# A list scheduler with new prices and a spare tile in three rings: attention and a gated channel mixer on one core

## The chip, the cores and the metric

The kernel runs on one core of a Trainium2 chip, with its five engines: TensorE (PE), VectorE (DVE), ScalarE (ACT), GpSimd (POOL) and SyncE (SP, which issues DMAs). The metric is the device time in microseconds; lower is better. Weights, inputs and the output lie in HBM.

## The reference

Attention with RMS-normalised q and k, then a channel mixer: tokens are blended with the token before, a squared ReLU and a sigmoid gate follow. B = 8, H = 12, S = 448, head size 64, D = 768, F = 1024, all float32 (the mixer's weights come as float64).

```python
def rmsnorm(x, g):
    return x / np.sqrt(np.mean(x * x, axis=-1, keepdims=True) + 1e-06) * g
q_n, k_n = rmsnorm(q, g_q), rmsnorm(k, g_k)
attn = softmax(1/sqrt(64) * q_n @ k_n.T)            # per batch and head
x = (attn @ v) laid out as (B, S, 768)
x_prev = x shifted by one token, zeros first
xk = mu_k * x + (1 - mu_k) * x_prev
xr = mu_r * x + (1 - mu_r) * x_prev
k = np.maximum(xk @ w_k, 0.0)
out = sigmoid(xr @ w_r) * (k * k @ w_v)
```

## The kernel before

All large products run in f16 as a high and a low part, three products for one (high by high, high by low, low by high). Work on attention goes by quads of heads: there are 24 quads `u` (three for each batch). `load` brings q and k, `stats` forms the norms (square on ScalarE, half the sum on GpSimd, the rest and a Newton inverse root on VectorE), `preps` scales, splits and transposes them into `stk`: for the first PE_T = 6 quads by TensorE's transposition through a PSUM bank (`turn`), later by a transposing DMA issued by SyncE. `scores` takes 7 groups for each quad; a group takes two of the 5 banks of the ring `sc`, and `expo` runs twice on it: VectorE finds the negated maximum, ScalarE the exponential with its sum in an accumulator. `probs` waits for both, forms the reciprocals and spawns two `split`s: ScalarE writes the high part into a `nat` tile, VectorE the low part and gives the score bank back. A transposing DMA then writes it to `pT`; ten early groups go by TensorE's transposition instead (`probs_pe`). `attends` multiplies with v and writes `x`.

The mixer follows, one batch at a time: `mix` blends two tokens (GpSimd into a `df` tile, VectorE onto it, ScalarE's high part, GpSimd's low part), `moe` runs the products, `square` forms the squared ReLU (ScalarE into a `kf` tile, ScalarE's square, GpSimd's square and low part), `gate` and `store` make the output tile `o`. `weights` and `wsplit` turn the float64 weights into two f16 parts; the staging tiles `wf` and `raw` of this work lie in a pool of their own. When the first `o` tile is taken, `late()` closes that pool and opens another in its place.

The order of every engine's instructions is not written by hand: each of these routines is a thread that yields instructions, and `Plan` is a list scheduler that emits them. It keeps a planned clock for each engine, the planned end of each use of a tile, and prices (`price`, and in `emit` those of DMAs and of TensorE's groups). In each step `run` takes, from all threads, the instruction with the smallest key: the later of its engine's clock and the end of what it depends on, less a tenth of its thread's priority. The emitted order is the order of the engine's queue. A thread that needs a tile of a `Ring` waits until one is free. Before the change, a VectorE instruction with no operand in PSUM is held in the plan until 190 ns before the planned end of the last GpSimd instruction emitted. A transposition on TensorE is priced 300 ns (`TR_COST`). The rings `nat`, `df` and `kf` have 4, 2 and 2 tiles (`NAT_BUFS`, the `df` ring's own figure and `KF_BUFS`).

Every instruction is recorded at one line of the profile, L256 (the call in `emit`), so groups are told apart by their tiles.

Of the kernel before, what the change touches and what calls it, by code (L numbers as in the profile page):

```python
# [87 lines left out]
LEAD_W = 1  # L88
PE_P = range(1, 21, 2)
SC_KEEP = 2  # L90
TR_COST = 300
W_GAP = 10e3
W_PUSH = 0.03
NEWTON_ON = "DVE"
# [1 line left out]
DMA_SLOW = 1.0  # L96
DMA_SHARE = 1.0
PE_SLOW = 1.0
F64_EXP = 2.0 ** -112
F64_NEG = -2.0 ** 32  # L100

# [45 lines left out]
def width(x):  # L147
    n = 1
    for _, c in x.ap[1:]:
        n *= c  # L150
    return n


def in_psum(x):
    return "PSUM" in str(x.tensor.space)
# [37 lines left out]
class Plan:  # L193
    LAT = 35

    def __init__(self, tc):
        self.tc = tc
        self.clk = dict.fromkeys(("PE", "DVE", "ACT", "POOL", "SP"), 0.0)
        self.last, self.use, self.threads = {}, {}, []
        self.form, self.dma_free, self.pool_end, self.n = None, {"SP": 0.0, "ACT": 0.0}, 0.0, 0  # L200

    def margin(self, form):
        if form == "moe":
# [46 lines left out]
    def emit(self, ops):  # L250
        e = ops[0].eng
        rel = self.ready(ops)
        s = max(self.clk[e], rel)
        for op in ops:
            with self.tc.issue_after(self.last[e].ins) if e in self.last else nullcontext():
                r = op.fn(op.kw["out"], op.kw["value"]) if op.fn.__name__ == "memset" else op.fn(**op.kw)  # L256
            self.last[e] = r
        if e == "PE":
            form, cost = ops[0].form
            form = MODE.get(form, 0)  # L260
            cost *= PE_SLOW
            if form != self.form:
                s += 105
            self.form = form
            self.clk[e] = s + cost
            fin = s + cost + 190
            for op in ops:
                self.note(op, fin)
        elif ops[0].fn.__name__.startswith("dma"):
            op = ops[0]  # L270
            x = op.kw["out"]
            n = width(x) * x.ap[0][1]
            if "transpose" in op.fn.__name__:
                w, iss, tot = n / 128 * 1.21, 1510, 4000
            else:
                w, iss, tot = n / 55, 600, 3300
            w, tot = w * DMA_SLOW, tot * DMA_SLOW
            other = "ACT" if e == "SP" else "SP"
            if e == "ACT":
                end = s + (375 if n > 60000 else 610)  # L280
            else:
                end = max(s + iss, min(self.dma_free[e] - 1200, s + 4000))
            self.clk[e] = end + 35
            begin = max(self.dma_free[e], s + tot - w - 900)
            both = DMA_SHARE * min(w, max(0.0, self.dma_free[other] - begin))
            self.dma_free[e] = begin + w + both
            self.dma_free[other] += both
            self.note(op, self.dma_free[e] + 900)
        else:
            op = ops[0]  # L290
            pace, dur = (x * OP_SLOW for x in price(op))
            if e == "DVE" and not any(in_psum(x) for x in op.kw.values() if isinstance(x, bass.AP)) and width(op.kw["out"]) > 2:
                s = max(s, self.pool_end - 190)
            self.clk[e] = s + pace
            if e == "POOL":
                self.pool_end = s + dur
            self.note(op, s + dur)
        self.n += 1

    def run(self):  # L300
        while self.threads:
            best, key = None, None
            for th in list(self.threads):
                if not isinstance(th[2], list):
                    if not th[2]():
                        continue
                    self.advance(th)
                    if th not in self.threads or not isinstance(th[2], list):
                        continue
                slack = self.margin(th[2][0].form[0]) if th[2][0].eng == "PE" else 0  # L310
                mode = MODE.get(th[2][0].form[0], 0) if th[2][0].eng == "PE" else None
                wait = SWITCH if mode == 0 and self.form else 0
                k = max(self.clk[th[2][0].eng] + wait, th[3] + slack) - PS * (th[1]() if callable(th[1]) else th[1])
                if best is None or k < key:
                    best, key = th, k
            if best is None:
                if any(isinstance(th[2], list) or th[2]() for th in self.threads):
                    continue
                assert not self.threads, [(th[0].__name__, th[2]) for th in self.threads]
                break  # L320
            r = self.ready(best[2])
            if r > best[3] + 1:
                best[3] = r
                continue
            self.emit(best[2])
            self.advance(best)


class Ring:
    def __init__(self, pool, shape, dtype, name, n, plan):  # L330
        self.pool, self.shape, self.dtype, self.name, self.plan = pool, shape, dtype, name, plan
        self.free, self.of, self.lent = ["%s%d" % (name, k) for k in range(n)], {}, {}

    def lend(self, owner, views):
        self.free = views + self.free
# [9 lines left out]
    def get(self, early=False):  # L345
        ok = lambda: [x for x in self.free if early or isinstance(x, str)]
        while not ok():
            yield ok
        tag = ok()[0]
        self.free = [x for x in self.free if x is not tag]  # L350
        if not isinstance(tag, str):
            self.of[id(tag)] = (tag, None, tag)
            return tag
        pool = self.pool() if callable(self.pool) else self.pool
        t = pool.tile(self.shape, self.dtype, name=tag, bufs=1)
        name = aps(t).tensor.name
        self.of[id(t)] = (tag, name, t)
        old = self.plan.use.get("slot " + tag)
        if old:
            self.plan.use[name, 0], self.plan.use[name, 1] = [(0, 1 << 30, old, True, False)], [(0, 1 << 30, old, True, False)]  # L360
        return t
# [27 lines left out]
def attn_moe_kernel(tc, q, k, v, g_q, g_k, mu_k, mu_r, w_k, w_v, w_r, out):  # L389
# [13 lines left out]
    T, V, A, G_, SP = (Engine(n, e) for n, e in (("PE", nc.tensor), ("DVE", nc.vector), ("ACT", nc.scalar), ("POOL", nc.gpsimd), ("SP", nc.sync)))  # L403
# [26 lines left out]
    st = {"wdone": 0, "g": 0, "moe": 0, "vl": 0, "gm": False, "mus": False, "want": "xk", "sg": 0, "su": 0, "pu": 0, "vi": 0, "wkeys": 0, "kdone": 0, "zq": 0, "tq": 0, "lu": 0}  # L430
# [7 lines left out]
    def until(f):  # L438
        while not f():
            yield f  # L440
# [4 lines left out]
    late_pool = []  # L445

    def late():
        if not late_pool:
            bctx.close()
            late_pool.append(ctx.enter_context(tc.tile_pool(name="late", bufs=1)))  # L450
        return late_pool[0]

    R = {
        "qk": Ring(ap_, [P, 2, S], F32, "qk", QK_BUFS, plan),
        "nat": Ring(ap_, [P, 2 * NT, P], F16, "nat", NAT_BUFS, plan),
        "stk": Ring(ap_, [P, 2, 2 * NT, P], F16, "stk", STK_BUFS, plan),
        "vh": Ring(ap_, [P, 2 * NSL, HD], F16, "vh", VH_BUFS, plan),
        "vl": Ring(ap_, [P, 2 * NSL, HD], F16, "vl", VH_BUFS, plan),
        "x": Ring(ap_, [P, NT + 1, HD], F32, "x", X_BUFS, plan),
        "xk": Ring(mp, [P, ND, 2, S], F16, "xk", 1, plan),  # L460
        "df": Ring(mp, [P, S], F32, "df", 2, plan),
# [469 lines left out]
    def wsplit(nm, kt, c, ci, f):  # L931
# [24 lines left out]
        st["wdone"] += 1  # L956
        st["wkeys"] += ci < NF
        if ci < NF and st["wkeys"] == NF:
            yield V.tensor_reduce(out=wsc[:, 0:1], in_=WSC[:, 0:NF], axis=AX.X, op=ALU.min)
            yield V.tensor_scalar(out=RSC, in0=WIN[:, 0:NF], scalar1=wsc[:, 0:1], scalar2=RELU_SCALE, op0=ALU.mult, op1=ALU.mult)  # L960
            yield V.tensor_reduce(out=wsc[:, 1:2], in_=WIN[:, 0:NF], axis=AX.X, op=ALU.max)
            yield V.scalar_tensor_tensor(out=wsc[:, 1:2], in0=wsc[:, 1:2], scalar=1.0 / RELU_SCALE, in1=smu[:, 0:1], op0=ALU.mult, op1=ALU.mult)
            st["rsc"] = True
        if st["wdone"] == NW:
            yield V.tensor_scalar(out=WIN[:, NF:NF + ND], in0=WIN[:, NF:NF + ND], scalar1=smu[:, 1:2], scalar2=0.5, op0=ALU.mult, op1=ALU.mult)
            yield V.tensor_scalar(out=WIN[:, NF + ND:NW], in0=WIN[:, NF + ND:NW], scalar1=wsc[:, 1:2], scalar2=0.5, op0=ALU.mult, op1=ALU.mult)
            yield V.tensor_scalar(out=WIN[:, NF + ND:NW], in0=WIN[:, NF + ND:NW], scalar1=wsc[:, 1:2], scalar2=None, op0=ALU.mult)
            st["wout"] = True
# [141 lines left out]
```

## Time and profile before

| | before |
|---|---|
| median of 3 runs | 1060.49 us (1059.37 to 1060.85) |
| the profiled execution's own time | 1058.49 us |
| its span | 1056.7 us |
| mean granted TensorE clock | 0.953 |
| busy PE / DVE / ACT / POOL | 925.9 / 802.9 / 770.7 / 675.8 us |
| the 16 DMA engines, HBM read and written | 50.40 and 11.01 MB |

The profile shows one execution. Busy time is the time in which an engine has an instruction under way; register, branch and DMA-issuing instructions do not count. A wait is the idle time of an engine ahead of an instruction, put down to what released it last. In a row of a group, `out<-in` names the tiles (buffer numbers left out), followed by the shapes and the count, then the busy time in us and the mean duration in ns, then the idle time just before these instructions and its releasers. In a row of one tile the three figures are the least, middle and greatest duration in ns, followed by the first and the last start in us. `x126` is a count. In the rows by stage the engines' busy times stand in the order PE, PEld (weight load), DVE, ACT, POOL, followed by the granted clock, the DMA engines' share and GB/s.

### The profile page before, as it was taken

The page shows a single profiled execution, that of the slowest core. Times are in us where ns is not written, and L with a number is a line of the kernel's source. Part 1 is how long each engine was busy: PE and PEld are TensorE (multiplying, and loading weights), DVE is VectorE, ACT ScalarE, POOL GpSimd, SP SyncE. Part 2 cuts the span into 40 slices and gives each one's busy share as a digit, 9 for nine tenths or more (in the row PEclk, how much of TensorE's full clock was granted, in tenths as well). Part 3 has the DMA queues.
Part 4 walks back from the last instruction along what each step waited for, and adds up shares of the span by engine and source line. Part 5 has one row for each costly group of instructions (what it writes and reads, how often), then busy time and mean ns, then how long its engine had stood idle before and what let it go on. Part 6 is the DMA issues. An engine that isn't in the chain of part 4 may idle for free. (4 is left out here: it accounts for less than half of the span.)

```text
span 1056.7 us, 19126 instructions
## 1 busy us (share of the span) xinstructions
PE 925.9 (88%) x6185; PEld 488.9 (46%) x6185; DVE 802.9 (76%) x2034; ACT 770.7 (73%) x1786; POOL 675.8 (64%) x716
## 2 busy tenths in 40 slices
PE   1667666889988999998989999999899999999997
PEld 1334323444544555454534455455445554455564
DVE  5888899898699688868997897959876898673100
ACT  3687877888679788877788787868787888773311
POOL 2575579655588576874698457857695569725711
PEclk9567878899999999999999999999999999999999
DMA  6865557876877899778976998679887898753011
GB/s 172 196 145 123 136 140 189 176 145 134 178 134 146 163 172 165 155 149 148 176 160 129 181 174 165 136 143 183 151 152 153 165 179 164 135 89 79 1 31 30
DMA packets 467108, 151.68 MB, mean 144 GB/s; under 512 B 438848, under 2 KB 463424, under 8 KB 467008
## 3 DMA queue, kind: packets, MB, share of 16 engines
q1 hardware_dynamic: 447472, 132.47, 66.1%
q10 hardware_dynamic: 19536, 18.00, 5.9%
q8 instruction: 48, 0.79, 0.3%
q14 instruction: 52, 0.43, 0.1%
HBM read 50.40 MB, written 11.01 MB: 58 GB/s over the span
## 5 line engine op out<-in xcount | busy, mean ns | idle before, releaser
L256 PE MATMUL mm<-wvh,kk 128*128 128x384 f16 x896 | 233.3, 326 | 0.5 <-DVE o L256 0.5
L256 ACT ACTIVATE sc<-sc,sums 128x448 f32<-128x448 f32 x316 | 192.2, 611 | 54.1 <-DVE sums L256 47.1
L256 DVE SCALAR_TENSOR_TENSOR nat<-sc,sums,nat 128x448 f16<-128x448 f32 x306 | 199.8, 676 | 37.0 <-ACT nat L256 35.3
L256 PE MATMUL mm<-xk,wkh 128*128 128x448 f16 x768 | 213.1, 359 | 9.7 <-DVE WSC L256 5.7
L256 ACT ACTIVATE nat<-sc,sums 128x448 f16<-128x448 f32 (+1 forms) x326 | 194.9, 646 | 25.8 <-DVE sums L256 10.4
L256 DVE TENSOR_REDUCE sums<-sc 128x1 f32<-128x448 f32 x336 | 193.6, 614 | 21.9 <-PE sc L256 21.3
L256 PE MATMUL mm<-wrh,xr 128*128 128x384 f16 x672 | 177.1, 326 | 0.0
L256 PEld LDWEIGHTS <-kk 128*128 128x128 f16 (+1 forms) x1362 | 129.5, 98 | 97.2 <-issue 15.6
L256 PE MATMUL sc<-stk 64*128 64x448 f16 (+1 forms) x1152 | 128.3, 369 | 34.4 <-DVE nat L256 19.4
L256 PE MATMUL mm<-wvl,kk 128*128 128x384 f16 x448 | 146.0, 326 | 0.0
L256 PE MATMUL mm<-xk,wkl 128*128 128x448 f16 x384 | 137.8, 359 | 0.0
L256 PE MATMUL ot<-pT,vh 128*64 128x448 f16 x768 | 122.4, 376 | 17.3 <-DMA pT<-nat 8.0
L256 PEld LDWEIGHTS <-xr 128*128 128x128 f16 x1008 | 95.6, 98 | 73.4 <-issue 13.1
L256 DVE SCALAR_TENSOR_TENSOR df<-x,bsc,df 128x448 f32<-128x448 f32 x96 | 108.3, 1137 | 25.3 <-POOL df L256 25.0
L256 PEld LDWEIGHTS <-wkh 128*128 128x128 f16 x768 | 72.8, 99 | 83.9 <-issue 25.5
L256 PE MATMUL mm<-wrl,xr 128*128 128x384 f16 x336 | 109.5, 326 | 0.0
L256 PEld LDWEIGHTS <-stk 64*128 64x128 f16 (+1 forms) x1152 | 43.5, 99 | 103.3 <-issue 68.5
L256 POOL TENSOR_TENSOR o<-o,bsc 128x384 f32<-128x384 f32 x48 | 43.8, 913 | 69.5 <-DVE o L256 57.0
L256 POOL TENSOR_TENSOR nat<-nat 128x448 f32<-128x448 f32 x46 | 53.9, 1171 | 50.6 <-ACT nat L256 45.4
L256 POOL TENSOR_TENSOR qk<-qk,ss 128x896 f32<-128x896 f32 x36 | 62.5, 1737 | 34.5 <-DVE ss L256 28.8
L256 DVE SCALAR_TENSOR_TENSOR o<-o,mm 128x384 f32<-128x384 f32 x56 | 30.6, 546 | 70.2 <-PE mm L256 70.2
L256 POOL TENSOR_TENSOR nat<-qk,nat 128x896 f16<-128x896 f32 x36 | 67.8, 1883 | 23.4 <-ACT nat L256 23.3
(141 smaller groups left out, 1632.6 us busy)
## 6 DMA issues: line engine op xcount, KB each, us to landing
out_dram<-o SPq DMA_DIRECT2D x56, 192.0 KB, 3.3
qk<-in_k_dram SPq DMA_DIRECT2D x46, 224.0 KB, 4.0
qk<-in_q_dram SPq DMA_DIRECT2D x108, 64.0 KB, 2.5
vf<-in_v_dram SPq DMA_DIRECT2D x96, 64.0 KB, 2.8
raw<-in_moe_w_v_dram ACTq DMA_DIRECT2D x12, 512.0 KB, 4.7
vf<-in_v_dram SPq DMA_DIRECT2D x96, 48.0 KB, 2.5
raw<-in_moe_w_r_dram ACTq DMA_DIRECT2D x12, 384.0 KB, 3.7
kk<-in_moe_w_k_dram ACTq DMA_DIRECT2D x8, 384.0 KB, 4.0
```

Source lines behind the costliest of these rows:

```text
L256: r = op.fn(op.kw["out"], op.kw["value"]) if op.fn.__name__ == "memset" else op.fn(**op.kw)
```

## The change

The change alters the planner's prices and gives three rings one more tile each from the opening of the late pool on. No instruction's kind or number is altered; the order in which they are emitted may be.

- An ACT instruction with an accumulator that follows another such one is put 130 ns later in the plan (`ACC_GAP`), and 130 ns are added to its key when the next instruction is chosen.
- VectorE and GpSimd now hold each other in the plan. For each, the last 16 planned instructions that use SBUF are kept; an instruction that would start inside one of the other engine's starts 190 ns before its end. VectorE's instructions with an operand in PSUM, or not wider than 2 elements, still take no part.
- `TR_COST` goes from 300 to 130, the planned issue of a transposing DMA from 1510 to 1600 ns, of another DMA on SyncE from 600 to 640 ns.
- `Ring.grow` adds tiles; `late()` gives one more to `kf`, `df` and `nat`.
- `wsplit` waits for the mixing scales (`mus`) and for `rsc` before it forms products of them.

```diff
-TR_COST = 300
+TR_COST = 130
...
+ACC_GAP = 130
+LATE_BUFS = (("kf", 1), ("df", 1), ("nat", 1))
...
-                w, iss, tot = n / 128 * 1.21, 1510, 4000
+                w, iss, tot = n / 128 * 1.21, 1600, 4000
             else:
-                w, iss, tot = n / 55, 600, 3300
+                w, iss, tot = n / 55, 640, 3300
...
-            if e == "DVE" and not any(in_psum(x) for x in op.kw.values() if isinstance(x, bass.AP)) and width(op.kw["out"]) > 2:
-                s = max(s, self.pool_end - 190)
+            if e == "ACT":
+                acc = op.kw.get("accum_out") is not None
+                if acc and self.acc:
+                    s = max(s, self.clk[e] + ACC_GAP)
+                self.acc = acc
+            if e == "POOL" or e == "DVE" and not any(in_psum(x) for x in op.kw.values() if isinstance(x, bass.AP)) and width(op.kw["out"]) > 2:
+                for a, b in self.held["DVE" if e == "POOL" else "POOL"]:
+                    if a <= s < b - 190:
+                        s = b - 190
+                h = self.held[e]
+                h.append((s, s + dur))
+                del h[:-16]
             self.clk[e] = s + pace
-            if e == "POOL":
-                self.pool_end = s + dur
...
+                if self.acc and th[2][0].eng == "ACT" and th[2][0].kw.get("accum_out") is not None:
+                    wait += ACC_GAP
...
+    def grow(self, pool, n):
+        for _ in range(n):
+            tag = "%sx%d" % (self.name, len(self.more))
+            self.more[tag] = pool
+            self.free.append(tag)
...
-        pool = self.pool() if callable(self.pool) else self.pool
+        pool = self.more.get(tag) or (self.pool() if callable(self.pool) else self.pool)
...
             late_pool.append(ctx.enter_context(tc.tile_pool(name="late", bufs=1)))
+            for name, n in LATE_BUFS:
+                R[name].grow(late_pool[0], n)
...
         if ci < NF and st["wkeys"] == NF:
+            yield from until(lambda: st["mus"])
...
         if st["wdone"] == NW:
+            yield from until(lambda: st.get("rsc"))
```

More of the change, by code (lines that the diff above doesn't have):

```diff
@@ L199, in __init__ @@
         self.last, self.use, self.threads = {}, {}, []
-        self.form, self.dma_free, self.pool_end, self.n = None, {"SP": 0.0, "ACT": 0.0}, 0.0, 0
+        self.form, self.dma_free, self.acc, self.n = None, {"SP": 0.0, "ACT": 0.0}, False, 0
+        self.held = {"DVE": [], "POOL": []}
     def margin(self, form):
@@ L331, in __init__ @@
         self.pool, self.shape, self.dtype, self.name, self.plan = pool, shape, dtype, name, plan
-        self.free, self.of, self.lent = ["%s%d" % (name, k) for k in range(n)], {}, {}
+        self.free, self.of, self.lent, self.more = ["%s%d" % (name, k) for k in range(n)], {}, {}, {}
+    def grow(self, pool, n):
[3 more added lines that the diff above has]
+            self.free.append(tag)
     def lend(self, owner, views):
```

## The prediction

> **Where the time goes before.** I read the page first (shares, then the forty slices), then busy time by stage, then TensorE's waits in the long middle stage, then single groups and tiles.
>
> ```profile
> span 1056.7 us, 19126 instructions
> PE 925.9 (88%) x6185; PEld 488.9 (46%) x6185; DVE 802.9 (76%) x2034; ACT 770.7 (73%) x1786; POOL 675.8 (64%) x716
> ...
> PE   1667666889988999998989999999899999999997
> ...
> PEclk9567878899999999999999999999999999999999
> ...
> PE 17%; DVE 11%; POOL 7%; ACT 5%; DMA 5%; issue 4%; SPq 0%; POOLq 0%; ACTq 0%; DVEq 0%
> ```
>
> TensorE is busy 88% of the span and in the last four fifths of it never far from full; the granted clock (PEclk, tenths) is low only in the first fifth. The chain of waits names many owners with small shares: no single wait carries the time.
>
> ```profile
> core 0: us, PE busy (x) PEld busy (x) DVE busy (x) ACT busy (x) POOL busy (x), PEclk, DMA share, GB/s
> 0.00:26.00 26.00, 3.46 (x16) 2.66 (x17) 13.84 (x52) 8.55 (x15) 6.26 (x16) 1.00 0.68 173
> 26.00:211.00 185.00, 125.97 (x761) 66.89 (x760) 163.93 (x456) 141.85 (x312) 126.03 (x145) 0.74 0.68 158
> 211.00:264.00 53.00, 47.78 (x351) 25.23 (x350) 48.26 (x144) 46.50 (x110) 27.94 (x29) 1.00 0.70 140
> 264.00:964.00 700.00, 661.67 (x4554) 344.26 (x4552) 563.87 (x1366) 551.64 (x1299) 479.40 (x487) 1.00 0.82 155
> 964.00:1057.00 93.00, 87.03 (x514) 49.82 (x510) 12.95 (x19) 22.19 (x52) 36.14 (x40) 0.99 0.08 22
> ```
>
> Three stages. From 26 to 211 us, while the weights are prepared, VectorE bounds: 163.93 of 185 us, TensorE only 125.97 at a granted clock of 0.74. From 264 to 964 us TensorE bounds: 661.67 of 700, so 38.3 us of idle is all that a better order can win there. From 964 us on the last batch's products run alone on TensorE, 87.03 of 93 us. So a change of order has two places to act: the start, by VectorE's queue, and the 38.3 us in the middle. What makes up the latter:
>
> ```profile
> engine line waited for: us in total, times, longest us
> PE sc L256 <- DVE nat L256: 13.9, 24, 1.8
> PE ot L256 <- DMA pT<-nat: 7.7, 9, 1.9
> ...
> PE mm L256 <- POOL xk L256: 2.2, 1, 2.2
> ```
>
> The largest, 13.9 us in 24 waits, is the next scores waiting for a score bank that VectorE's subtraction of the split (`nat`) gives back.
>
> **The change, part by part.** All of it but the spare tiles only alters the planner's clocks, so no instruction is added or removed; each engine gets another order of the same work.
>
> *Accumulations.* The planner adds 130 ns where an ACT instruction with an accumulator follows another, in the choice of the next work too. ScalarE's own timeline in the middle stage shows what such a neighbour costs (columns: start, duration):
>
> ```profile
> 702.49 0.61 ACT L256 ACTIVATE sc<-sc,sums 128x448 f32<-128x448 f32 x1 [2.42 <-DVE sums L256]
> 703.03 0.14 ACT L256 ACTIVATION_READ_ACCUMULATOR sc<-sc,sums 128x1 f32 x1
> 703.20 0.61 ACT L256 ACTIVATE sc<-sc,sums 128x448 f32<-128x448 f32 x1
> ...
> 703.78 0.61 ACT L256 ACTIVATE sc<-sc,sums 128x448 f32<-128x448 f32 x1
> ...
> 704.49 0.61 ACT L256 ACTIVATE sc<-sc,sums 128x448 f32<-128x448 f32 x1
> ...
> 705.07 0.64 ACT L256 ACTIVATE nat<-sc,sums 128x448 f16<-128x448 f32 x1
> ```
>
> From start to start: 0.71, 0.58, 0.71, 0.58 us. The two exponentials of one group (they write their sums into the same bank) cost 0.13 us more; the first of the next group does not, although it too follows an accumulation, and costs what the plain instruction at 705.07 does. So the price is right for half of the neighbours and invented for the other half. All 158 pairs could stand so: 158 x 0.13 = 20.5 us of ScalarE at most. It is filled only where another ScalarE instruction is ready within 130 ns; I take half, 10 us. ScalarE has 148 us of idle in the middle stage (700 - 551.64), and holds 5% of the chain against 73% busy, so I let 5/73 of it count: **-0.7 us**; ends 0 and -10, and above nothing what the second rival says. Queued behind the displaced exponential are its group's sum, reciprocal and two splits; TensorE's scores wait for these.
>
> *Spare tiles.* `nat` goes from 4 to 5 tiles, `df` and `kf` from 2 to 3, once the first `o` tile is taken:
>
> ```profile
> L256 ACT ACTIVATE o<-mm,bsc x144: 347/372/422, 240.0 to 1047.7; 128x128 f32<-128x128 f32 x144
> ...
> L256 DVE SCALAR_TENSOR_TENSOR wvl<-wf,WSC,wvh x6: 1276/1285/1716, 180.3 to 228.7; 128x1024 f16<-128x1024 f32 x6
> ```
>
> That is from 240.0 us, after the last reader of the weights' staging memory, in which they lie, started at 228.7 us; so no new wait at the hand-over. What they can take away, in ScalarE's waits from 211 to 964 us:
>
> ```profile
> ACT nat L256 <- DMA pT<-nat: 9.8, 10, 2.9
> ...
> ACT nat L256 <- DMA stk<-nat: 6.1, 7, 1.4
> ...
> ACT kf L256 <- POOL kk L256: 1.1, 2, 0.9
> ```
>
> A `nat` write that waits for the transposing DMA to have read the tile before is a ring too short: 15.9 us in 17 waits, 0.94 us each. Behind each stand a split and VectorE's subtraction, which gives back the score bank. TensorE's waits for that are 0.58 us each (13.9 / 24); if every one of the 17 stood behind one of them, 17 x 0.58 = 9.9 us would go. I take about 0.6 of it, **-6 us**, since next in line after the tile is the same DMA (7.7 us of TensorE's waits for pT are its landing, which a tile does not shorten); ends 0 and -13.9. `kf` shows 1.1 us of waiting and `df` none on ScalarE: TensorE's 2.2 us for xk is the most that earlier mixing can bring. **-1 us**, ends -3.3 (1.1 + 2.2) and +2, the latter if GpSimd, given more products to choose from, lets the statistics of the next quad stand once for about two of its instructions.
>
> *Turns in SBUF.* Until now only VectorE was held, until the end of the GpSimd instruction planned last, even one that starts later. Now each is held by an instruction of the other that has begun. What a collision costs:
>
> ```profile
> L256 DVE SCALAR_TENSOR_TENSOR df<-x,bsc,df x96: 659/1050/2574, 147.3 to 984.0; 128x448 f32<-128x448 f32 x96
> L256 POOL TENSOR_TENSOR nat<-qk,nat x36: 1872/1882/1892, 256.9 to 918.0; 128x896 f16<-128x896 f32 x36
> L256 DVE TENSOR_REDUCE sst<-nat x46: 592/610/621, 15.4 to 898.0; 128x14 f32<-128x448 f32 x46
> L256 POOL TENSOR_TENSOR kf<-kf x64: 922/932/1382, 173.2 to 997.8; 128x448 f32<-128x448 f32 x64
> ...
> L256 DVE SCALAR_TENSOR_TENSOR df<-x,bsc,df 128x448 f32<-128x448 f32 x12 | 13.5, 1136 | 2.1 <-POOL df L256 2.0
> ...
> L256 DVE SCALAR_TENSOR_TENSOR vl<-vf,bstat,vh 128x512 f16<-128x512 f32 x8 | 8.4, 1050 | 0.0
> ...
> L256 DVE SCALAR_TENSOR_TENSOR vl<-vf,bstat,vh x48: 734/970/2018, 21.9 to 931.7; 128x512 f16<-128x512 f32 x48
> ```
>
> The mixing instruction alone takes 659 ns and at worst 2574, which is itself and one whole GpSimd subtraction (659 + 1882 = 2541); GpSimd's squares go from 922 to 1382. The Trainium skill (SBUF — State Buffer, section "SBUF: two separate sides") says that whichever of the two starts first has the shared pair of ports for the whole instruction and the other blocks fully; the 2574 agrees. The same section limits this on VectorE's side to two-port modes and two SBUF inputs, and this case's one-input reduction, 592 to 621 ns over 46, is indeed never lengthened: the change holds GpSimd in the plan for it without cause. If that decides, the term below becomes 0. Where VectorE bounds, from 26 to 211 us, the excess is 12 x (1136 - 659) = 5.7 us for mixing and 8 x (1050 - 734) = 2.5 us for `vl`, 8.2 us in all. The turns are not in the key by which work is chosen, so collisions are counted, not avoided; only truer clocks can help. **-2 us**, a quarter; ends -8.2 and +8.2 (they may as well double). In the middle stage the excess lies on engines with idle time: nothing, as long as VectorE stays at its 563.87 of 700; without that cover it would be up to 84 x (1137 - 659) ns, 40 us.
>
> *Transposition, 300 to 130 ns.* It touches the start alone (those from `nat` end at 238 us):
>
> ```profile
> L256 PE MATMUL sc<-ident,nat x140: 272/353/477, 20.2 to 237.8; 128*128 128x128 f32 x140
> ...
> L256 PE MATMUL sc<-ident,nat 128*128 128x128 f32 x126 | 27.6, 361 | 13.3 <-DVE nat L256 5.4 <-POOL nat L256 2.5 <-DVE xk L256 2.3
> 120.24 1.09 PE L256 MATMUL sc<-ident,nat 128*128 128x128 f32 x4 [0.91 <-DVE xk L256]
> L256 ACT ACTIVATE stk<-sc,gc x12: 569/644/713, 21.7 to 227.5; 128x512 f16<-128x512 f32 x6, 128x384 f16<-128x384 f32 x6
> L256 ACT CAST pT<-sc 128x512 f16<-128x512 f32 (+1 forms) x20 | 10.8, 543 | 1.1 <-PE sc L256 0.6 <-DVE bstat L256 0.3
> ```
>
> 126 of them keep TensorE busy 27.6 us, 219 ns each; four take 1.09 us to the last result. The old plan has 4 x 300 + 190 = 1.39 us (0.30 late), the new 4 x 130 + 190 = 0.71 us (0.38 early). ScalarE waits little for them now (0.6 us over 20 copies to pT). There are 24 groups for stk (the 12 scaled ones shown and as many plain) and 20 for pT, half of them of 4 and half of 3, 154 transposes in all; 44 x 0.38 = 16.7 us of waiting at the head of ScalarE's queue is the most; VectorE's queue, the bound there, stands behind ScalarE's copy. Since queues are mostly behind, I take an eighth: **+2 us**; lower end -5, as TensorE's planned clock loses up to 154 x 170 ns of which the excess over 219 ns, 154 x 81 = 12.5 us, was wrong, and less than half can matter where TensorE is not the bound.
>
> *DMA issue (1510 to 1600, 600 to 640 ns) and the two guards.*
>
> ```profile
> L256 SPq DMA_TRANSPOSE stk<-nat x36: 1339/1617/3248, 259.8 to 920.1; - x36
> ```
>
> The middle transposing issue takes 1617 ns of SyncE's queue, so its price comes nearer; the DMAs themselves are the same, so I take 0, ends -1 and +1. The guards only forbid reading scales before they are written, add no instruction, and cost 0 unless the new order would have come to them early; the wait would then stand on a weights' thread, not on an engine.
>
> **Sum.** -0.7 - 6 - 1 - 2 + 2 = -7.7 us on the profiled execution's 1058.49 us (span 1056.7): 1050.8. The median of the runs, 1060.49, lies 2.0 above that execution, so the forecast is **1052.8 us**.
>
> **Rivals.**
> *Nothing moves (1060 us).* A filler between two exponentials delays the second by its own 0.64 us less the 0.13 saved, 0.51 us; at 79 pairs 40 us of longer held score banks. If a fifth reaches TensorE's waits for `nat`, 8 us, the gain is gone. For it: the group at 703.78 shows that half the price is imaginary, so fillers are put where they save nothing. Against: ScalarE's queue often holds a split that is due anyway.
> *Slower (1069 us).* The transposition is priced too low: half of the 16.7 us on VectorE's path at the start, 8.4, and no gain behind it. It decides once ScalarE's and VectorE's waits for transposed banks before 240 us pass about 8 us. For it: 219 ns against 130. Against: 0.6 us of wait today, and backlog on both queues.
> The Trainium skill (TensorE: Matmul & The Clock Gate, "Part 4: PE-mode transpose") gives about 275 ns for one in a kernel, and says that transposes do not count as activity for the clock; an estimate by that page is 154 x 145 ns = 22 us of under-pricing and a start that stays at low clock, as the 0.74 above agrees with.
> *Much faster (1038 us).* The fifth `nat` tile takes all 13.9 us of bank waits and true clocks the 8.2 us excess: 1060.5 - 22.1 = 1038.4.
>
> **Chances.** Forecast 0.42, much faster 0.15, nothing moves 0.17, slower 0.26. About 0.2% (2.1 us) is what a measurement here tells from no change, so faster is below 1058.4: 0.57; within: 0.17; slower: 0.26. The range 1038 to 1069 reaches the fast and the slow rival's times and leaves out about 0.2; the forecast's own is 1046 to 1058, from the ends of the tile term.
>
> **What would show it.** Right: ScalarE's waits of `nat` for pT and stk under 5 us, TensorE's for VectorE's `nat` under 8 us between 264 and 964 us, TensorE's idle there near 31 us, and the stretch to 211 us ending with as much TensorE work done. Pairs of exponentials 0.58 us apart, or with an instruction between, in about half of the groups. Wrong: TensorE's work before 211 us smaller, ScalarE waiting for transposed banks, VectorE's df median above 1050 ns, or waits of scores grown through fillers. As every order after the first difference is new, a scatter that none of the parts owns can also decide; it is inside the range.

## Result: 0.5% slower, less than the scatter of orders

| | before | after |
|---|---|---|
| median of 13 runs | 1060.85 us | 1066.8 us |
| ratio to before, 95% interval | | 1.0050 [1.0036, 1.0063] |
| span of the profiled execution | 1056.7 us | 1064.9 us |
| busy PE / DVE / ACT / POOL | 925.9 / 802.9 / 770.7 / 675.8 us | 926.4 / 807.1 / 768.0 / 676.0 us |

The forecast was 1052.8 us, faster; the kernel became slower by about 6 us. The page of the kernel after:

```profile
span 1064.9 us, 19096 instructions
...
PE 926.4 (87%) x6185; PEld 488.3 (46%) x6185; DVE 807.1 (76%) x2034; ACT 768.0 (72%) x1786; POOL 676.0 (63%) x716
...
PE   1566667779999999999699999999798999999997
...
PEclk9678868989999999999899999999899999999999
...
PE 19%; issue 2%; DVE 1%; DMA 1%; POOL 1%; ACT 1%; SPq 1%; POOLq 0%; ACTq 0%; DVEq 0%
```

TensorE's work is the same to 0.5 us; 7.7 us more of its idle make the difference (138.5 against 130.8). The new slices show a few holes (a 6 and a 7 in the middle), with the granted clock down in the slice of the first and just behind the second. By stage:

```profile
core 0: us, PE busy (x) PEld busy (x) DVE busy (x) ACT busy (x) POOL busy (x), PEclk, DMA share, GB/s
26.00:211.00 185.00, 124.89 (x797) 67.58 (x798) 163.29 (x457) 143.31 (x319) 129.33 (x148) 0.79 0.68 155
211.00:264.00 53.00, 46.16 (x315) 24.59 (x315) 48.82 (x143) 44.50 (x102) 23.94 (x24) 0.90 0.78 147
264.00:964.00 700.00, 657.48 (x4509) 339.22 (x4504) 568.35 (x1371) 550.13 (x1300) 480.13 (x490) 0.99 0.82 154
964.00:1065.00 101.00, 95.27 (x563) 54.83 (x561) 13.61 (x21) 22.03 (x53) 36.95 (x40) 1.00 0.09 24
```

At 211 us TensorE is ahead of before, by the number of products (the x behind its busy time, which counts its transpositions too). From 211 to 264 us it loses that (315 against 351), and from 264 to 964 us it does 45 fewer (4509 against 4554), so that 563 instead of 514 are left for the end, where nothing hides. TensorE's waits from 264 to 964 us, first one row of before, then after:

```profile
PE ot L256 <- ACT vh L256: 6.9, 5, 2.8
```

```profile
PE ot L259 <- ACT vh L259: 15.8, 12, 4.6
PE sc L259 <- DVE natx L259: 7.3, 3, 5.4
PE sc L259 <- DVE nat L259: 5.2, 11, 1.0
...
PE ot L259 <- DMA pT<-nat: 1.3, 2, 0.9
...
PE ot L259 <- DMA pT<-natx: 0.6, 1, 0.6
```

(The spare tiles are named `natx`, `dfx`, `kfx`.) Waits for a score bank went from 13.9 to 12.5 us (`nat` and `natx` together), those for the transposing DMA from 7.7 to 1.9, and those for ScalarE's work on v rose from 6.9 to 15.8. That work (`vh`) is in most of these waits the square of v, whose sums a product of TensorE takes up; the longest, 4.6 us, is for v's high part. ScalarE's own waits of `nat` for these DMAs, from 211 to 964 us, were 15.9 us and are 1.3:

```profile
ACT nat L259 <- DMA stk<-nat: 0.8, 2, 0.4
ACT nat L259 <- DMA pT<-nat: 0.5, 1, 0.5
```

That reads like a local trade. The experiments show that an order moved by a price that says nothing does as much.

### The profile page after: what moved, and what is told of

Its sections match the earlier page's. It is cut to its first block, busy times and chain, and to the rows that moved or that the text cites. A ratio compares the mean times of both kernels' runs of the same rounds, so it can differ in the third digit from the quotient of the medians.

```text
span 1064.9 us, 19096 instructions
## 1 busy us (share of the span) xinstructions
PE 926.4 (87%) x6185; PEld 488.3 (46%) x6185; DVE 807.1 (76%) x2034; ACT 768.0 (72%) x1786; POOL 676.0 (63%) x716
## 5 line engine op out<-in xcount | busy, mean ns | idle before, releaser
L259 DVE SCALAR_TENSOR_TENSOR nat<-sc,sums,nat 128x448 f16<-128x448 f32 x254 | 166.1, 676 | 26.4 <-ACT nat L259 25.9
L259 ACT ACTIVATE nat<-sc,sums 128x448 f16<-128x448 f32 (+1 forms) x268 | 161.8, 656 | 13.5 <-DVE sums L259 6.2
L259 ACT ACTIVATE o<-mm,bsc 128x128 f32<-128x128 f32 x144 | 45.2, 381 | 57.5 <-PE mm L259 43.4
L259 POOL TENSOR_TENSOR nat<-nat 128x448 f32<-128x448 f32 x42 | 49.2, 1172 | 57.9 <-ACT nat L259 50.1
L259 PE MATMUL ot<-pT,vl 128*64 128x448 f16 x384 | 74.9, 382 | 4.9 <-DVE vl L259 4.9
```

## Experiments

Two theories stood at the start. **Parts:** the loss belongs to one part of the change. **Order:** the change acts through the order of the queues; each small change of a price gives another order of nearly all instructions, and before was a good one among many. All ratios are to the kernel before, timed beside it on the same chip, with 95% intervals.

### The spare tiles, in the old order and in a free one

For the first run the thread that the planner before picks at each of its 5769 steps was written down, and the new planner follows that list:

```diff
+LATE_BUFS = (("kf", 1), ("df", 1), ("nat", 1))
...
+        for k in seq:
...
+                best = [th for th in self.threads if th[4] == names[k] and isinstance(th[2], list)]
...
+            self.emit(best[0][2])
...
-                if best is None or k < key:
-                    best, key = th, k
```

> The order in which the kernel before emits its instructions is kept, instruction by instruction on every engine; only the three rings get their spare tile. Theory tiles (the prediction's term): ScalarE's waits of nat for pT and stk (15.9 us from 211 to 964) nearly vanish and the time falls by 3 to 8 us, to 1053 to 1058. Theory order (all that the change does, it does through the order): the waits vanish and the time moves by no more than 2 us, since TensorE's queue is in the same order and waits for something else next.

Measured: 0.9991 [0.9971, 1.0012], no change that can be told. TensorE's waits of this run from 264 to 964 us, and ScalarE's from 211 to 964 us:

```profile
PE sc L265 <- DVE nat L265: 13.3, 15, 2.9
...
PE ot L265 <- ACT vh L265: 6.5, 5, 2.8
...
PE sc L265 <- DVE natx L265: 1.4, 3, 0.6
```

```profile
ACT nat L265 <- DMA pT<-nat: 9.7, 4, 4.5
```

The same tiles with the planner free to choose:

> The spare tiles alone, with the planner free to choose its order and all its old prices. Theory tiles: -3 to -8 us, as with the order kept. Theory order: the sign can't be told ahead; the time differs from that with the order kept by 3 us or more.

Its waits of TensorE from 264 to 964 us:

```profile
PE ot L260 <- ACT vh L260: 16.7, 13, 4.2
PE sc L260 <- DVE nat L260: 14.1, 17, 4.4
...
PE sc L260 <- DVE natx L260: 1.7, 4, 0.6
```

In the old order ScalarE's 17 waits became 4, but longer ones (9.7 us in all; that the queue now comes sooner to the next thing that is not ready is one reading, not tested). TensorE's bank waits stayed, 14.7 us. Not quite as theory order had it (the waits did not vanish), but the time does what it said. With the planner free the same three tiles cost 1.0104 [1.0075, 1.0133], +11 us. The only difference between these two kernels is the order.

### One price at a time

Each is the kernel before with one part of the diff. These runs, and all with a moved price below, also hold the two guards of `wsplit`; one of them, the old planner with DMAs 0.1% cheaper, emits TensorE's first 4206 of 6185 products in the order of before, so the guards do not move the old order there. The new issue prices of DMAs were not timed alone.

> Only the 130 ns for neighbouring accumulations (price and key), no spare tiles, other prices old. Theory fillers (the prediction's rival): the pairs of exponentials go from about 169 to about 110 neighbours, ScalarE saves some 6 us of gaps, a group's sum comes 0.5 us later, and the time rises by 3 to 8 us. Theory order: within 8 us of before on either side, and not tied to the gaps saved.

> Only the turns of VectorE and GpSimd in SBUF, other prices old, no spare tiles. Theory turns: the mean of VectorE's mixing falls from 1137 ns towards 1000 and the time by 2 us or more. Theory order: the mean may fall or not, the time is within 8 us of before on either side and not tied to it.

> Only TensorE's transposition at 130 ns, other prices old, no spare tiles. Theory transposition (the prediction's slower rival): ScalarE's waits for transposed banks before 211 us pass 8 us, and TensorE stands at 264 us at least 5 us of work behind the kernel before (fewer than 1100 products against 1128). Theory order: the waits may pass 8 us, but TensorE is within 3 us of work of before at 264 us; what the time loses or gains by its end, anything from -10 to +25 us, comes after it.

Measured: accumulations 1.0102 [1.0066, 1.0137], turns 1.0115 [1.0081, 1.0150], transposition 1.0116 [1.0096, 1.0135]. Each of these parts alone, and the tiles alone, cost more than all together. Theory order's own 8 us on either side were passed too. The accumulations' neighbours fell from 169 pairs of exponentials to 115, as theory fillers had it, but its 3 to 8 us were 11. With the turns the mean of VectorE's mixing fell from 1137 to 1025 ns, and the time rose. In the run of the transposition both signs of theory transposition came: ScalarE waited 8.8 us for transposed banks from 26 to 211 us, and TensorE stood at 1075 products at 264 us, fewer than 1100; theory order's "within 3 us of work" did not hold. Yet up to 211 us TensorE had done more than before (825 products against 774):

```profile
26.00:211.00 185.00, 128.91 (x809) 70.23 (x808) 160.59 (x441) 141.68 (x318) 126.34 (x142) 0.76 0.61 144
211.00:264.00 53.00, 38.43 (x250) 20.95 (x250) 48.16 (x143) 42.02 (x92) 19.89 (x25) 0.74 0.79 167
```

Its loss lies behind that: 250 products from 211 to 264 us against 351, at a clock of 0.74. TensorE waits there up to 5.1 us for VectorE's step of the last weights, whose last low part starts at 246.3 us instead of 228.7:

```profile
PE mm L260 <- DVE wf L260: 7.2, 3, 5.1
```

```profile
L260 DVE SCALAR_TENSOR_TENSOR wvl<-wf,WSC,wvh x6: 1276/1284/1630, 202.4 to 246.3; 128x1024 f16<-128x1024 f32 x6
```

So the count fell behind the stage in which the named waits lie. VectorE did stand 3.3 us more in that stage (busy 160.59 us against 163.93); whether that or the new order put the weights back by 17.6 us was not tested.

### Prices that say nothing

If single parts all cost about 11 us, what does a change cost that carries no information? The planner before got one price 0.1% higher or lower:

```diff
-OP_SLOW = 1.0
+OP_SLOW = 1.001
```

`OP_SLOW` scales the prices of all VectorE, ScalarE and GpSimd instructions; `DMA_SLOW` and `PE_SLOW` do the same for the planned durations of DMAs and of TensorE's groups.

> None of the change; the planner's prices of all VectorE, ScalarE and GpSimd instructions are 0.1% higher, which says nothing new of the chip. Theory parts (the 10 us of each part alone come from what the part says): the time stays within 2 us of before. Theory order (the order before is a lucky draw, and any other order costs): the time rises by 3 to 13 us, like that of the parts alone.

> The same with prices 0.1% lower. Theory parts: within 2 us of before. Theory order: 3 to 13 us more, not the mirror image of 0.1% higher.

> The same with the planned durations of the DMAs 0.1% higher. Theory parts: within 2 us of before. Theory order: 3 to 13 us more.

> The same with the planned durations of TensorE's groups 0.1% higher. Theory parts: within 2 us of before. Theory order: 3 to 13 us more.

All four are slower: 1.0044, 1.0114, 1.0249 and 1.0065, three of them by the 3 to 13 us of theory order, one by 25. That one, with 0.1% on the DMAs' prices, waits for score banks:

```profile
PE sc L260 <- DVE nat L260: 26.6, 27, 3.6
```

These waits are 12.7 us longer than before's. The rest lies elsewhere: its span is 32.5 us longer (1089.2 against 1056.7), of which 18.0 us are TensorE's busy time for the same products (943.9 against 925.9), at a granted clock of 0.97 instead of 1.00 from 264 to 964 us.

The order before is a favourable one: of the six moved orders of its planner that were timed in the end, four are slower, two the same, and none is measurably faster. The same was then done to the whole change.

> The whole change, with the planner's prices of VectorE, ScalarE and GpSimd instructions 0.1% higher. Theory draw (the change trades one lucky order for an ordinary one, and does nothing on average): the four such versions of the change lie like those of before, between +4 and +25 us on the kernel before, with a mean near +11 us. Theory better prices (the new prices and tiles help any order by some us, and only the luck of the old one hides it): their mean is 4 us or more below the +11 us of the four on the old planner. Theory worse prices: their mean is 4 us or more above it.

> The whole change, with those prices 0.1% lower. As for 0.1% higher: the mean of the four is compared with +11 us.

> The whole change, with the planned durations of the DMAs 0.1% higher. As for the others of the four.

> The whole change, with the planned durations of TensorE's groups 0.1% higher. As for the others of the four.

> The old planner, with the planned durations of TensorE's groups 0.1% lower. Theory average gain (the change lowers the time of an ordinary order by about 0.9%): between +4 and +25 us, around +12. Theory no average gain: anywhere from -10 to +25 us; the mean of the old planner's orders comes down to that of the new one's.

> The old planner, with the planned durations of the DMAs 0.1% lower; TensorE's order parts from that of before only after two thirds of its instructions. Both theories: the first two thirds take the same time to within 1 us; the end costs 0 to 8 us, less than where the order parts early.

> The whole change, with the planned durations of TensorE's groups 0.1% lower. Theory average gain: between -10 and +13 us on the kernel before, around +3. Theory no average gain: around +11 us.

> The whole change, with the planned durations of the DMAs 0.1% lower. Theory average gain: between -10 and +13 us on the kernel before, around +3. Theory no average gain: around +11 us.

Products of TensorE are counted as in the rows by stage; the last two columns are TensorE's waits from 264 to 964 us, for score banks (`nat` and `natx`) and for ScalarE's work on v.

| planner | price moved | ratio to before | products to 211 | 211 to 264 | 264 to 964 | bank waits, us | v waits, us |
|---|---|---|---|---|---|---|---|
| old | none (before) | 1 | 774 | 351 | 4554 | 13.9 | 6.9 |
| old | engines +0.1% | 1.0044 [1.0019, 1.0070] | 770 | 353 | 4509 | 12.7 | 13.2 |
| old | engines -0.1% | 1.0114 [1.0098, 1.0130] | 793 | 328 | 4462 | 24.0 | 5.9 |
| old | DMA +0.1% | 1.0249 [1.0217, 1.0282] | 772 | 334 | 4341 | 26.6 | 5.0 |
| old | TensorE +0.1% | 1.0065 [1.0038, 1.0092] | 772 | 350 | 4511 | 15.1 | 12.4 |
| old | TensorE -0.1% | 0.9984 [0.9958, 1.0011] | 792 | 341 | 4544 | 12.2 | 11.9 |
| old | DMA -0.1% | 1.0015 [0.9996, 1.0034] | 761 | 346 | 4556 | 10.7 | 5.6 |
| new | none (after) | 1.0050 [1.0036, 1.0063] | 808 | 315 | 4509 | 12.5 | 15.8 |
| new | engines +0.1% | 0.9907 [0.9871, 0.9943] | 797 | 314 | 4607 | 4.4 | 16.8 |
| new | engines -0.1% | 1.0034 [1.0013, 1.0055] | 829 | 275 | 4562 | 14.7 | 6.4 |
| new | DMA +0.1% | 1.0016 [0.9992, 1.0040] | 739 | 317 | 4579 | 3.9 | 9.8 |
| new | TensorE +0.1% | 1.0115 [1.0084, 1.0145] | 800 | 285 | 4488 | 10.1 | 16.9 |
| new | TensorE -0.1% | 1.0196 [1.0173, 1.0219] | 818 | 292 | 4407 | 5.5 | 39.3 |
| new | DMA -0.1% | 0.9890 [0.9875, 0.9904] | 808 | 315 | 4615 | 1.8 | 16.2 |

(The old planner with DMAs 0.1% cheaper keeps before's order on TensorE for the first two thirds; it parts least and, with the -0.1% on TensorE, costs nothing.)

After four orders on each side theory better prices held: the new planner's lay 1.6 us above before in the mean, the old planner's 11.4 (differences of medians). Two more on each side took that away, and theory average gain failed on three of the four: -2.3 us where it had +4 to +25, +21.8 and -11.1 where it had -10 to +13.

The mean of the six moved orders of the old planner is 1.0079, with a standard deviation of 0.009; that of the seven of the new one 1.0030, with 0.011. The difference, -0.5%, has a standard error of 0.6% (the root of 0.009 squared / 6 + 0.011 squared / 7): whether the change helps an ordinary order stays open. The orders of a side are not independent either, so that error is rather too small: five of the old planner's seven, before among them, have one and the same order on TensorE up to 257 us at least, and a sixth joins them up to 217 us. What is settled is the size of the scatter, about 10 us for one order, against a change of 6.

The clearest pair is after and its version with DMAs 0.1% cheaper. That version has the lowest ratio of the table, a median of 1050.25 us against 1061.39 of before beside it, and beats both kernels. Its stages, and TensorE's waits from 264 to 964 us:

```profile
211.00:264.00 53.00, 46.16 (x315) 24.73 (x317) 48.79 (x143) 44.52 (x102) 23.95 (x24) 0.90 0.77 147
264.00:964.00 700.00, 673.70 (x4615) 347.85 (x4611) 569.68 (x1380) 553.73 (x1312) 491.77 (x503) 0.99 0.82 155
```

```profile
PE ot L259 <- ACT vh L259: 16.2, 11, 3.9
...
PE sc L259 <- DVE nat L259: 1.6, 3, 1.0
```

Up to 264 us the two agree to the product (808 and 315); TensorE's order is the same up to 307 us. From there 0.1% on a price is worth 106 products: 673.70 us of work against 657.48.

Two shifts show in the means of the seven orders on each side, though the single orders overlap. Bank waits average 16.5 us on the old planner and 7.6 on the new. The waits for v average 8.7 and 17.3, so in the mean what was gained there is given back here (-8.9 and +8.6). But the second figure leans on the worst of the new orders; without it the mean is 13.7. Its row, TensorE waiting from 264 to 964 us:

```profile
PE ot L259 <- ACT vh L259: 39.3, 19, 12.8
```

Nothing here shows that the spare tiles do either. With the tiles alone the bank waits are 14.7 us in the old order and 15.8 in a free one, no less than the 13.9 of before; and the waits for v are 6.5 us in the old order, 16.7 in the free one, while three moved orders without any spare tile have 11.9 to 13.2.

From 211 to 264 us the new planner has done 275 to 317 products in each of its orders, the old 328 to 353, without an overlap; ahead of it the new is in front in the mean (800 against 776), so the start costs 18 products, or 2.6 us at 661.67 / 4554 us each. The transposition alone (250) and the turns alone (290) show it, the accumulations (340) and the tiles (341) do not. As five of the seven old figures come from one order of TensorE, this is less than seven against seven; those five spread from 341 to 353 by themselves.

### The sums of a group, written elsewhere

With the order of before kept, the accumulators go to SBUF:

```diff
-        yield A.activation(out=sp[:, 0:S], in_=sp[:, 0:S], func=AF.Exp, bias=sums[:, j:j + 1], accum_out=both[0][:, S + j:S + j + 1])
+        yield A.activation(out=sp[:, 0:S], in_=sp[:, 0:S], func=AF.Exp, bias=sums[:, j:j + 1], accum_out=sums[:, 4 + j:5 + j])
...
-        yield V.tensor_scalar(out=r, in0=both[0][:, S:S + 2], scalar1=1e-9, scalar2=2.0 ** -15, op0=ALU.add, op1=ALU.mult)
+        yield V.tensor_scalar(out=r, in0=sums[:, 4:6], scalar1=1e-9, scalar2=2.0 ** -15, op0=ALU.add, op1=ALU.mult)
```

> The order of before kept, instruction by instruction; the accumulators of all exponentials are written to the small SBUF tile instead of the group's first score bank, and VectorE reads them there. Theory bank (the second exponential of a group waits because its sum goes into the bank that the first one has just written): the two starts come to 0.64 us or less, as between groups. Theory accumulator (a pair of neighbours costs it whatever is written): 0.70 us stays. The time itself moves by less than 3 us either way, since ScalarE is not what TensorE waits for most.

ScalarE's timeline, then VectorE's instruction that reads the sums (its least, middle and greatest duration, with the reciprocal behind it and the row of before, and its group):

```profile
702.21 0.64 ACT L264 ACTIVATE sc<-sc,sums 128x448 f32<-128x448 f32 x1
702.73 0.24 ACT L264 ACTIVATION_READ_ACCUMULATOR sc<-sc,sums 128x1 f32 x1
702.82 0.65 ACT L264 ACTIVATE sc<-sc,sums 128x448 f32<-128x448 f32 x1
...
703.43 0.68 ACT L264 ACTIVATE kf<-mm,RSC 128x448 f32<-128x448 f32 x1
```

```profile
L264 DVE TENSOR_SCALAR sums<-sums x168: 150/169/2060, 34.9 to 975.1; 128x2 f32<-128x2 f32 x168
L264 DVE RECIPROCAL sums<-sums x168: 144/155/167, 36.8 to 975.9; 128x2 f32<-128x2 f32 x168
```

```profile
L256 DVE TENSOR_SCALAR sums<-sc x158: 133/152/163, 34.5 to 954.1; 128x2 f32<-128x2 f32 x158
```

```profile
L264 DVE TENSOR_SCALAR sums<-sums 128x2 f32<-128x2 f32 x168 | 70.2, 419 | 12.9 <-ACT sc L264 12.0 <-ACT nat L264 0.5
```

The exponentials of a group now start 0.61 us apart, and so does what follows: 160 of 165 pairs without idle time between them lie at 0.60 to 0.63, where before 129 of 164 lay between 0.66 and 0.76. Theory accumulator is out. Theory bank fits, but it is not the bank as such that delays. A trace also records on which semaphores an instruction waits, and before, 128 of those 129 second exponentials wait for ScalarE's own semaphore, which the accumulator read ahead of them raises. They start 32 ns after that read has ended, in the middle. The 33 that follow at 0.58 us have no such wait and start while the read is still running, as at 703.78 in the timeline of before:

```profile
703.73 0.14 ACT L256 ACTIVATION_READ_ACCUMULATOR sc<-sc,sums 128x1 f32 x1
703.78 0.61 ACT L256 ACTIVATE sc<-sc,sums 128x448 f32<-128x448 f32 x1
```

With the sums in SBUF, 157 of the 160 have no such wait. So the 130 ns are a wait that the program holds where both sums go to one PSUM bank; whether the bank would delay the second one without it, no run shows.

The expectation for the time does not hold: 1.0198 [1.0170, 1.0226], +21 us. The two-element instruction on the sums takes 419 ns in the mean instead of 160 (24.0 us over 158 and 2.8 over 10 before), at worst 2060, 43 us over the kernel. Read from SBUF, it too waits for GpSimd's instructions: of the 96 that start while GpSimd has an instruction under way 71 take over 250 ns, of the 72 others none. The score banks come back later (TensorE's bank waits in the middle stage are 25.0 us).

## Why the prediction was wrong, step by step

- **What bounds (right).** TensorE bounds from 264 us on, VectorE before. The 38.3 us named as all that order can win there was the right pot: the moved orders leave between 25.5 and 52.6 us of idle in it, and the kernel after 42.5 instead of the 31 expected.
- **The sum (the step that failed).** It started from 1058.49 us as if that were what the planner gives, and added what each part changes. But a price is not applied to an order; it makes a new one, and the old order was itself a favourable one. On the old planner moves that say nothing cost from -0.2% to +2.5%, in the mean +0.8%, 8 us. Against that the terms of -0.7, -6, -1, -2 and +2 us were no forecast of one order. The scatter was named in the prediction's last sentence, given no size and called inside the range; its size was the answer. That the 1066.8 us lie in the range is luck: two moved orders, at 1083 and 1087 us, do not.
- **Accumulations (reading right, term irrelevant).** That only the second exponential of a group pays was right. Its cause is the wait for the accumulator read of the first, which the program holds where both sums go to one bank; the last run takes it away. The planner's part alone cost 11 us, not -0.7; the planner indeed made room where nothing is paid as well as where it is. How much of the 11 us is fillers and how much the new order, the runs do not separate.
- **Spare tiles (first sign right, the rest of the path wrong).** ScalarE's waits fell below the 5 us given as the sign, to 1.3. TensorE's bank waits did not follow: -6 us was taken and under 8 given as the sign; they fell by 1.4, to 12.5. Over the orders of the whole change they fell by 8.9 us in the mean, but with the tiles alone not at all. The prediction named the DMA's landing as late next; in this kernel it was v, where 8.9 us came back. In a kept order the term was 0 (-3.1 to +1.3 us by the interval), at the top end of its range. `kf` and `df`: nothing that could be told apart.
- **Turns (-2 taken).** Mixing did get shorter from 26 to 211 us, 1013 ns in the mean against 1136, and `vl` 797 against 1050, so the 8.2 us of excess became 4.8. But VectorE is as busy there as before, 163.29 us, and in the run of the turns alone the time rose by 10 us: shorter instructions brought nothing by themselves.
- **Transposition (+2 taken).** The mechanism named came: ScalarE's waits for transposed banks from 26 to 211 us rose fourfold, past the 8 us from which they were to decide. The rows, before and then after:

```profile
ACT stk L256 <- PE sc L256: 2.4, 3, 1.2
ACT pT L256 <- PE sc L256: 0.6, 1, 0.6
```

```profile
ACT stk L259 <- PE sc L259: 6.9, 7, 1.9
ACT pT L259 <- PE sc L259: 4.8, 5, 2.6
```

  VectorE waited for these copies in turn, 8.8 us against 0.8 (before, then after):

```profile
DVE stk L256 <- ACT stk L256: 0.8, 2, 0.5
```

```profile
DVE stk L259 <- ACT stk L259: 5.4, 10, 1.2
DVE pT L259 <- ACT pT L259: 3.4, 3, 2.2
```

  These waits took the place of others, though: VectorE's idle time in the stage is 21.7 us against 21.1, and TensorE had done 808 products by 211 us, not fewer than 774. The price that is paid lies from 211 to 264 us, at the last weights, which the prediction did not look at; their last low part starts at 238.3 us instead of 228.7.
- **The rivals.** "Slower" by the transposition had the right sign and came nearest in time (1069 us), but that is luck: its waits came and did not slow the stage in which they lie. "Nothing moves" missed by 7 us; a give-back there was, at v, and not through fillers, as the bank waits did not grow. No rival said that the base itself is a favourable draw, the one that a planner with hand-set prices should have suggested.

## What to carry to other kernels

Where a scheduler makes the order, do not judge a change by one order: time a few that are moved by prices saying nothing, on both sides, before believing a difference smaller than their scatter (here about 1%). To learn what a buffer or a price is worth by itself, keep the old order by its recorded steps and change that one thing. And since such moves are cheap, they are also a search: two of the six moves of the new planner were about 1% faster than the kernel before.

## What the hardware showed unexpectedly

- An exponential with an accumulator does not hold up the next one: the next starts 0.58 us behind it (0.61 with the sum in SBUF), 90 ns before the read of the accumulator ends, in the middle. Only where the program makes it wait for that read is it 0.66 to 0.76 us. The read takes 140 ns in the median into PSUM and 200 ns into SBUF.
- A VectorE instruction on two elements in SBUF can take 2060 ns for its 150, when GpSimd is at work: size is no protection from the turns, and both planners leave such instructions out. The kind of instruction is: the reciprocal of the same two elements never takes over 167 ns, though 80 of its 168 start while GpSimd is at work. The Trainium skill (SBUF — State Buffer, "SBUF: two separate sides") says that the pair of ports is held for a whole instruction; the 2060 ns agrees. It starts 0.03 us behind a GpSimd instruction of 2.07 us and ends with it:

```profile
329.43 2.07 POOL L264 TENSOR_TENSOR qk<-qk,gq 128x896 f32<-128x896 f32 x1
```

```profile
329.46 2.06 DVE L264 TENSOR_SCALAR sums<-sums 128x2 f32<-128x2 f32 x1
```

- A hole can cost twice. In the kernel after, TensorE stood for 4.59 us ahead of 527.63 us, and the granted clock from 525 to 535 us was 0.50, where it is 1.00 behind:

```profile
527.63 0.58 PE L259 MATMUL ot<-pT,vh 128*64 128x448 f16 x2 [4.59 <-ACT vh L259]
```

```profile
525.00:530.00 5.00, 0.58 (x2) 0.13 (x2) 4.93 (x9) 3.62 (x7) 5.00 (x6) 0.50 0.67 120
530.00:535.00 5.00, 4.40 (x24) 1.97 (x26) 4.09 (x7) 0.42 (x2) 5.00 (x6) 0.50 0.84 171
535.00:540.00 5.00, 5.00 (x33) 2.40 (x30) 4.27 (x11) 4.62 (x13) 3.06 (x6) 1.00 1.26 172
```

  How much this costs a kernel is not shown: busy time for the same 6185 products lies between 924.9 and 943.9 us over the kernels, and the one with the most idle time, 147.7 us, has 932.5.
